# Relu² attention feeding a GELU feed-forward: attention regrouped into two slots per quad, one relu of each quad on VectorE, transposes of the head put later

## The chip, the cores and the metric

One core of a Trainium2 chip. The metric is the device time of one launch in microseconds (us), the median of several runs; lower is better. The engines are TensorE (PE), VectorE (DVE), ScalarE (ACT), GpSimd (POOL, here mostly the issuer of the loads) and SyncE (SP, the issuer of DMA transposes and of the stores).

## The reference

```python
# q, k, v: (8, 12, 448, 64) float32
scores = scale * np.matmul(q, k.transpose(0, 1, 3, 2))     # scale = 1/sqrt(64)
attn = np.maximum(scores, 0.0) ** 2 / S                    # S = 448
attn_out = np.matmul(attn, v)
x = attn_out.transpose(0, 2, 1, 3).reshape(8 * 448, 12 * 64)
h = x @ w_in                                               # (3584, 768) @ (768, 2048)
g = 0.5 * h * (1.0 + erf(h / np.sqrt(2)))
out = g @ w_out                                            # (3584, 2048) @ (2048, 768)
```

There is no softmax: the scores go through a relu and a square, so blocks of keys are independent until the value product sums them.

## The kernel before

**Tiles.** Everything is computed in bf16 with float32 sums. The 12 heads of a batch are three quads (`G = 3`, index g) of four heads. The 448 keys are seven blocks of 64 (`NK = 7`, index i). A *score step* `QK[b, g, i]` (`fn_qk`, L504) is four matmuls on 64x64 quarters of the array, one per head, into one PSUM tile `ps`. Its relu (`fn_relu`: L516 on ACT, L518 on DVE) makes `a_sq` out of it, and DVE squares that in place (L525). The *value product* `AV[b, g]` (L564) is 28 such matmuls over the seven squared blocks of a quad, into a PSUM tile `pav`, which two copies (L287 on DVE, L289 on ACT) put into `xT`. The feed-forward is made of atoms: F1 (`add_f1`, L611), six 128x128 matmuls into `psh` with a GELU on ACT after it (L623), and F2 (`add_f2`, L651), 16 matmuls into `pso`, copied by DVE to `osb` and stored by SP.

**Buffers.** `ps` and `pav` share a ring of three PSUM tiles (`w_pp`); `psh`, `pso` and the transposes' `tp` share two (`f_pp`).

**Order.** A planner in Python (`Scheduler`) fixes the order of instructions on each engine before the program is built, from modelled durations. Each operation has engines it may run on, dependencies, buffers that it needs and frees, and a bias; the earliest start plus bias is taken first. On the chip, each engine then runs its instructions in that order. The planner orders the head (batches 0 and 1) by itself. For the steady part (batches 2 to 7) PE's order is a list, `pe_q`: slots of attention, and between the slots feed-forward atoms. While batch b's attention runs, the atoms of *stage* b are F1 of batch b - 1 and F2 of batch b - 2, spread evenly over `per` slots. In `slots()`, a slot takes the value product that is ready, if any, and fills up with score steps: two units in the first slot, three in all others, so that 24 units of a batch make eight slots. The whole order of loads on POOL is a list too (`pool_q`).

**The head.** Batch 0 is done in two halves of the query columns. q and k of batches 0 and 1 are transposed on PE (`add_tq` L435, `add_tk` L410), those of later batches by DMA transposes, for which DVE first copies them into `pq` and `pk` (L371, L360). The q half that batch 0's second half needs is one load, issued after the first block of w_in. The transposes of that half have only a bias, `T_LATE`; those of batch 1 may not be planned before the last score step of batch 0's first half. On POOL a small copy, the gate (L479), waits until a batch's transposed q has landed before the next loads are issued; w_out's two loads stand behind the gate of batch 2.

**Copies for the next batch.** From batch 3 on, the `pk`/`pq` copies for batch b + 1 may start once the first score step of a given slot is done, `at(n)` with n counted from the stage's first slot: 5 for stage 2, 3 for stage 3, else 1. The DMA transposes of q's later parts wait for slot n + 1.

```python
sch.add(eng, fn_relu, [o1], need=("a",), frees=("w",), bias=bias, other=RELU_DVE)
...
for n, slot in enumerate(order):
    for kind, x in slot:
        pe_q.append(AV[x] if kind == "AV" else QK[x])
    if n < per * len(stage):
        ...
        while atoms and done < total * (n % per + 1) / per - 0.01:
```

Of the kernel before, what the change touches and what calls it, by code (L numbers as in the profile page):

```python
# [12 lines left out]
B, H, S, D = 8, 12, 448, 64  # L13
KC = 112
NC = S // KC
HC = NC // 2
HS = S // 2
KB = 64
NK = S // KB
NA = 14  # L20
HP = H // 2
G = H // 4
# [8 lines left out]
T_LATE = 0.2  # L31
# [11 lines left out]
DMA_LAT = 2.13  # L43
SWITCH = 0.09
LEAD = 5


def cols(half):
# [29 lines left out]
        return self.op.start  # L78


class Scheduler:


# [4 lines left out]
    def __init__(self, buffers):  # L88
# [2 lines left out]
        self.open, self.mode, self.dma = [], None, DMA_FREE  # L91
        self.landed = [0.0] * 8
        self.log = []

    def add(self, engines, fn, deps=(), **kw):
        op = Op(engines, fn, deps, **kw)
        self.open.append(op)
        return op
# [86 lines left out]
def kernel(  # L185
# [113 lines left out]
    def dma(fn, nbytes, deps=(), issues=1):  # L299
        op = sch.add((("POOL", 0.7 * issues, (nbytes, issues)),), lambda e: fn(), deps)  # L300
        pool_q.append(op)
        return op
# [4 lines left out]
    QK, SQ, AV, X, GL = {}, {}, {}, {}, {}  # L307
# [18 lines left out]
    def add_q(b, g0, g1, c0=0, c1=NC):  # L326
        o = dma(lambda: load_q(b, g0, g1, c0, c1), (g1 - g0) * 4 * KC * (c1 - c0) * 256, war(b))
        for g in range(g0, g1):
            for c in range(c0, c1):
                ld_q[b, g, c] = o  # L330

    def add_v(b, g0, g1):
        def fn():
            get_nat(b)
            nc.gpsimd.dma_start(vt[b][:, 2 * g0 : 2 * g1], kv_view(v, b, g0, g1))  # L335

        old = [o for (bb, *_), o in AV.items() if bb == b - 3]
        o = dma(fn, (g1 - g0) * 4 * S * 256, old)
        for g in range(g0, g1):
            ld_v[b, g] = [o]  # L340
# [6 lines left out]
    def add_win(i):  # L347
        m = sum(WINS[:i])
        c = slice(128 * m, 128 * (m + WINS[i]))
        o = dma(lambda: load_win(c), DM * 128 * WINS[i] * 4, issues=3)  # L350
        for x in range(m, m + WINS[i]):
            ld_win[x] = o
# [73 lines left out]
    def add_tq(b, g, c0=0, c1=NC, bias=T_BIAS, after=()):  # L426
        box, n = [], (c1 - c0) * KC

        def fn(e):
            tp = f_pp.tile([128, 2, n], BF16, tag="f", name="tp")  # L430
            box.append(tp)
            for j in range(2):
                for c in range(c0, c1):
                    for e in range(2):
                        nc.tensor.transpose(  # L435
                            tp[64 * e : 64 * e + 64, j, bass.ts(c - c0, KC)],
                            nq[b][:, 4 * g + 2 * e + j, bass.ts(c, D)],
                            ident[:KC, :KC],
                        )

        def fn2(e):
            copy(e, get_T(b)[0][:, 2 * g : 2 * g + 2, c0 * KC : c1 * KC], box[0])

        d = 0.125 * (c1 - c0)
        deps = [ld_q[b, g, c] for c in range(c0, c1)] + list(after)
        op = sch.add(
            (("PE", d, d + 0.22),), fn, deps, need=("f",), mode="T", bias=bias
        )
        ev = sch.add(e_copy(2 * n, 2), fn2, [op] + old_T(b), frees=("f",), bias=bias)
        for c in range(c0, c1):  # L450
            Tq[b, g, c] = (op, ev)
        return op
# [38 lines left out]
    def add_steps(todo, bias=0.0, dve=False):  # L491
        for blocks in todo:
            box = {}
            w = S if blocks[0][3] is None else HS
            used = w * len(blocks)

            def fn_qk(e_, blocks=blocks, box=box, w=w):
                ps = box["ps"] = w_pp.tile([128, 2, NB], F32, tag="w", name="ps")
                for x, (b, g, i, half) in enumerate(blocks):
                    qT, kT = get_T(b)  # L500
                    for e in range(2):
                        r = slice(64 * e, 64 * e + 64)
                        for j in range(2):
                            nc.tensor.matmul(  # L504
                                ps[64 * j : 64 * j + 64, e, x * w : x * w + w],
                                kT[r, g, i * 128 + 64 * j : i * 128 + 64 * j + 64],
                                qT[r, 2 * g + j, cols(half)],
                                start=True,
                                stop=True,
                            )  # L510

            def fn_relu(e_, box=box, used=used):
                box["a2"] = apool.tile([128, 2, S], BF16, tag="a", name="a_sq")
                ar, ps = box["a2"][:, :, :used], box["ps"][:, :, :used]
                if e_ == "ACT":
                    A.activation(ar, ps, AF.Relu, scale=c_att)  # L516
                else:
                    V.tensor_scalar(  # L518
                        ar, ps, c_att, 0.0,
                        op0=mybir.AluOpType.mult, op1=mybir.AluOpType.max,  # L520
                    )

            def fn_mul(e_, box=box, used=used):
                ar = box["a2"][:, :, :used]
                V.tensor_mul(box["a2"][:, :, :used], ar, ar)  # L525

            deps = []
            for b, g, i, half in blocks:
                cs = range(NC) if half is None else range(half * HC, half * HC + HC)
                deps += [Tk[b, g][1]] + [Tq[b, g, c][1] for c in cs]  # L530
            d = 0.19 * used / S
            o1 = sch.add((("PE", d, d + 0.24),), fn_qk, deps, need=("w",), mode="A", bias=bias)
            d = 0.19 + 0.00069 * 2 * used
            eng = (("ACT", d, d + 0.14),)
            if dve:
                d = 0.07 + 2 * used / 960
                eng += (("DVE", d, d + 0.12),)
            o2 = sch.add(
                eng, fn_relu, [o1], need=("a",), frees=("w",), bias=bias, other=RELU_DVE
            )  # L540
            d = 0.07 + used / 960
            o3 = sch.add((("DVE", d, d + 0.12),), fn_mul, [o2], bias=bias)
            for x, blk in enumerate(blocks):
                QK[blk] = o1
                SQ[blk] = (o3, box, x * w)
            for blk in blocks:
                if blk[2] == NK - 1:
                    add_av(blk, bias)
# [160 lines left out]
    def steps(b):  # L709
        return [((b, g, i, None),) for g in range(G) for i in range(NK)]  # L710
# [5 lines left out]
            tuple(x[n : n + 2]) for n in range(7, len(x), 2)  # L716
        ]

    def slots(todo, first):


        todo, ready, out = list(todo), [], []
        while todo or ready:
            slot, room = [], first if not out else 3
            new = []
            if ready:
                slot.append(("AV", ready.pop(0)))
            while todo and len(slot) < room:
                b, g, i, _ = todo.pop(0)[0]
                slot.append(("QK", (b, g, i, None)))  # L730
                if i == NK - 1:
                    new.append((b, g, None))
            ready += new
            out.append(slot)
        return out


    nc.scalar.dma_start(k32, kv_view(k, 0, 0, 1))
# [5 lines left out]
        out=ident, in_=ident, compare_op=mybir.AluOpType.not_equal, fill=1.0,  # L744
# [13 lines left out]
    for g in (1, 2):  # L758
        add_k(0, g, g + 1)
        add_q(0, g, g + 1, 0, HC)  # L760
        add_v(0, g - 1, g)
    add_v(0, 2, 3)
    add_win(0)
    add_q(0, 0, G, HC, NC)
    add_win(1)

    def landed(t):
# [20 lines left out]
        add_tk(0, g)  # L788
        add_tq(0, g, 0, HC)
    for g in range(G):  # L790
        add_tq(0, g, HC, NC, T_LATE)
    st0 = halves(0)
    add_steps(st0[:11], dve=True)
    add_steps(st0[11:], HALF_BIAS, True)
# [4 lines left out]
    add_load(1, 2, 3)  # L799
    add_win(4)  # L800
    for g in range(G):
        half = [order_only(QK[0, G - 1, NK - 1, 0])]
        add_tk(1, g, T_ONE, half)
        add_tq(1, g, bias=T_ONE, after=half)
    for m in range(0, KF, 2):
# [12 lines left out]
        add_f1(0, m, 1, bias=F1B_BIAS)  # L818


    todo = [x for b in range(2, B) for x in steps(b)]
    order = slots(todo, 2)
    first = [next((x for kind, x in sl if kind == "QK"), None) for sl in order]
    per = 8

    class at_slot:


        def __init__(self, n):
            self.key = first[n]  # L830

        @property
        def done(self):
            return QK[self.key].done
# [4 lines left out]
    stage = []  # L839
    add_load(3)  # L840
    for b in range(2, B):
        add_steps(steps(b))
        if b + 1 < B:

            n = per * (b - 2) + {2: 5, 3: 3}.get(b, 1)
            add_pk(b + 1, 0, G, after=at(n))
            add_pq(b + 1, 0, G, after=at(n))
            add_T_dma(b + 1, [at(n + (y >= 4)) for y in range(7)])
            if b + 2 < B:
                add_gate(b + 1)  # L850
                add_load(b + 2)
        x1, x2 = f1(b - 1), f2(b - 2)
        if b == 2:
            first_atoms = x1[:LEAD]
            stage.append(x1[LEAD:] + x2)
        else:
            stage.append(x2[:2] + mix(x1, x2[2:]))
    pe_q.extend(x[1] for x in first_atoms)
# [4 lines that stand above are left out]
            atoms = stage[n // per]  # L863
            if n % per == 0:
                total, done = sum(x[0] for x in atoms), 0.0
# [35 lines left out]
```

## Time and profile before

| what | us |
|---|---|
| device time, median of 3 runs | 399.45 |
| lowest and highest | 399.24, 400.35 |
| span in the profile | 398.9 |
| PE busy | 385.3 |
| ACT busy | 213.3 |
| DVE busy | 173.1 |

A page of the profile gives busy times of the engines over the span, rows of 40 equal slices, groups of equal instructions with their count, busy time and mean, and for each group what ended the idle time before it. Beside the page there are views of the same trace: a timeline (start, duration, engine, line, operation and tiles of merged instructions), windows (busy time of each engine in a stretch), waits, and a chain of waits. PE = matmuls, PEld = weight loads. Matmuls are pipelined and their ends are modelled; their starts are recorded.

### The profile page before, as it was taken

The page shows a single profiled execution, that of the slowest core. Times are in us where ns is not written, and L with a number is a line of the kernel's source. Part 1 is how long each engine was busy: PE and PEld are TensorE (multiplying, and loading weights), DVE is VectorE, ACT ScalarE, POOL GpSimd, SP SyncE. Part 2 cuts the span into 40 slices and gives each one's busy share as a digit, 9 for nine tenths or more (in the row PEclk, how much of TensorE's full clock was granted, in tenths as well). Part 3 has the DMA queues.
Part 4 walks back from the last instruction along what each step waited for, and adds up shares of the span by engine and source line. Part 5 has one row for each costly group of instructions (what it writes and reads, how often), then busy time and mean ns, then how long its engine had stood idle before and what let it go on. Part 6 is the DMA issues. An engine that isn't in the chain of part 4 may idle for free.

```text
span 398.9 us, 8136 instructions
## 1 busy us (share of the span) xinstructions
PE 385.3 (97%) x3497; PEld 215.8 (54%) x3497; DVE 173.1 (43%) x329; ACT 213.3 (53%) x323; POOL 45.2 (11%) x68
## 2 busy tenths in 40 slices
PE   7699999999999999999999999999999999999995
PEld 6477785455555555545555455545455555555552
DVE  3779961356544434634363433634343333110111
ACT  4878865774464654666546555556654646222200
POOL 8754204000200200020001000000000000000000
PEclk9879999999999999999999999999999999999998
DMA  9999966999895891897148921560111011110122
GB/s 178 187 203 204 199 100 109 212 203 217 140 204 115 118 200 35 155 158 116 41 90 131 187 60 41 113 106 2 41 30 51 2 41 41 39 28 14 41 79 79
DMA packets 69348, 42.95 MB, mean 108 GB/s; under 512 B 37696, under 2 KB 65728, under 8 KB 69312
## 3 DMA queue, kind: packets, MB, share of 16 engines
q0 software_dynamic: 30496, 22.47, 37.6%
q1 hardware_dynamic: 38544, 19.51, 23.4%
q8 instruction: 27, 0.44, 0.4%
q10 hardware_dynamic: 272, 0.46, 0.3%
q14 instruction: 9, 0.07, 0.1%
HBM read 45.61 MB, written 11.01 MB: 142 GB/s over the span
## 4 chain that ended last, share of the span: by engine, by line
PE 86%; DMA 4%; ACT 3%; DVE 2%; SPq 1%; POOL 1%; issue 1%; POOLq 0%; DVEq 0%; ACTq 0%
PE psh L611 36%; PE pso L651 35%; PE ps L504 8%; PE pav L564 7%; ACT a_sq L516 2%; DMA win_sb<-in_moe_w_in_dram 2%; DMA nk<-in_k_dram 2%; SPq L467 1%; DMA qT<-pq 1%; POOL v_sb L335 1%; DVE xT L287 0%; DVE a_sq L525 0%; DVE osb L287 0%; POOL nk L320 0%; PE tp L410 0%
## 5 line engine op out<-in xcount | busy, mean ns | idle before, releaser
L516 ACT ACTIVATE a_sq<-ps 128x896 bf16<-128x896 f32 (+1 forms) x161 | 140.7, 920 | 35.7 <-PE ps L504 35.7
L611 PE MATMUL psh<-xT,win_sb 128*128 128x448 bf16 (+1 forms) x864 | 156.1, 332 | 0.4 <-DVE osb L287 0.4
L651 PE MATMUL pso<-wout_sb,h_sb 128*128 128x384 bf16 x896 | 152.7, 326 | 0.0
L525 DVE TENSOR_TENSOR a_sq<-a_sq 128x896 bf16<-128x896 bf16 (+1 forms) x169 | 103.0, 621 | 104.9 <-ACT a_sq L516 104.8
L651 PEld LDWEIGHTS <-h_sb 128*128 128x128 bf16 x896 | 86.2, 98 | 63.6 <-issue 6.9
L611 PEld LDWEIGHTS <-win_sb 128*128 128x128 bf16 x864 | 80.7, 98 | 68.5 <-issue 13.6
L623 ACT ACTIVATE h_sb<-psh 128x448 bf16<-128x448 f32 x128 | 70.5, 551 | 68.2 <-PE psh L611 68.1
L287 DVE COPY osb<-pso 128x384 f32<-128x384 f32 x56 | 31.1, 556 | 77.3 <-PE pso L651 77.3
L504 PE MATMUL ps<-qT,kT 64*64 64x448 bf16 (+1 forms) x756 | 46.5, 339 | 2.4 <-ACT a_sq L516 1.6
L289 ACT CAST xT<-pav 128x448 bf16<-128x448 f32 (+1 forms) x26 | 12.9, 496 | 48.7 <-DVE xT L287 47.8
L564 PE MATMUL pav<-a_sq,v_sb 64*64 64x448 bf16 (+1 forms) x756 | 37.9, 339 | 0.4 <-ACT a_sq L516 0.4
L504 PEld LDWEIGHTS <-kT 64*64 64x64 bf16 x756 | 19.2, 107 | 22.1 <-issue 15.6
L287 DVE CAST xT<-pav 128x448 bf16<-128x448 f32 (+1 forms) x28 | 15.8, 566 | 29.7 <-PE pav L564 29.3
L564 PEld LDWEIGHTS <-v_sb 64*64 64x64 bf16 x756 | 20.3, 110 | 15.4 <-issue 7.6
L479 POOL COPY gate<-qT 128x4 bf16<-128x4 bf16 x5 | 0.9, 186 | 159.8 <-DMA qT<-pq 159.8
L236 POOL DMA_DIRECT2D nq<-in_q_dram x14 | 11.6, 827 | 1.5 <-DMA win_sb<-in_moe_w_in_dram 0.6
L335 POOL DMA_DIRECT2D v_sb<-in_v_dram x14 | 10.6, 761 | 3.3 <-DMA win_sb<-in_moe_w_in_dram 1.7
L320 POOL DMA_DIRECT2D nk<-in_k_dram x13 | 10.0, 769 | 5.0 <-DVE xT L287 2.0
L518 DVE TENSOR_SCALAR a_sq<-ps 128x896 bf16<-128x896 f32 x8 | 8.6, 1085 | 0.7 <-PE ps L504 0.7
L371 DVE COPY pq<-nq 112x512 bf16<-112x512 bf16 x36 | 8.3, 287 | 0.3 <-DMA nq<-in_q_dram 0.3
L435 PE MATMUL tp<-ident,nq 112*64 112x112 bf16 x96 | 4.2, 230 | 2.3 <-DMA nq<-in_q_dram 1.3
L360 DVE COPY pk<-nk 128x896 bf16<-128x896 bf16 x18 | 6.1, 386 | 0.0
(24 smaller groups left out, 42.3 us busy)
## 6 DMA issues: line engine op xcount, KB each, us to landing
nk<-in_k_dram POOLq DMA_DIRECT2D x5, 672.0 KB, 6.6
nq<-in_q_dram POOLq DMA_DIRECT2D x5, 672.0 KB, 9.3
v_sb<-in_v_dram POOLq DMA_DIRECT2D x5, 672.0 KB, 12.7
wout_sb<-in_moe_w_out_dram POOLq DMA_DIRECT2D x2, 1536.0 KB, 14.9
out_dram<-osb SPq DMA_DIRECT2D x8, 336.0 KB, 3.2
out_dram<-osb SPq DMA_DIRECT2D x8, 288.0 KB, 2.7
v_sb<-in_v_dram POOLq DMA_DIRECT2D x9, 224.0 KB, 8.0
out_dram<-osb SPq DMA_DIRECT2D x8, 240.0 KB, 2.7
```

Source lines behind the costliest of these rows:

```text
L236: nc.gpsimd.dma_start(nq[b][:, 4 * g0 : 4 * g1, c0 * D : c1 * D], q_view(b, g0, g1, c0, c1))
L287: V.tensor_copy(dst, src)
L289: A.copy(dst, src)
L320: nc.gpsimd.dma_start(nk[b][:, 2 * g0 : 2 * g1], kv_view(k, b, g0, g1))
L335: nc.gpsimd.dma_start(vt[b][:, 2 * g0 : 2 * g1], kv_view(v, b, g0, g1))
L504: nc.tensor.matmul(ps[64 * j : 64 * j + 64, e, x * w : x * w + w], kT[r, g, i * 128 + 64 * j : i * 128 + 64 * j + 64], qT[r, 2 * g + j, co ...
L516: A.activation(ar, ps, AF.Relu, scale=c_att)
L525: V.tensor_mul(box["a2"][:, :, :used], ar, ar)
L564: nc.tensor.matmul(pav[0][o2 : o2 + 64, e, :w], vt[b][r, 2 * g + e, bass.ts(i, D)], box["a2"][r, e, o : o + w], start=(i == 0), stop=(i == ...
L611: nc.tensor.matmul(ph[:, x * n : x * n + n], win_sb[:, kd, bass.ts(m + x, 128)], xT[b][:, kd, c], start=(kd == 0), stop=(kd == KD - 1),)
L623: A.activation(hT[b // 2][:, m : m + nm, o + c.start : o + c.stop], box[0][:, :S].rearrange("p (x n) -> p x n", x=nm), AF.Gelu,)
L651: nc.tensor.matmul(po[:, :ND], hT[pr][:, kf, bass.ts(t, 128)], wout_sb[:, kf, bass.ts(n, ND)], start=(kf == 0), stop=(kf == KF - 1),)
```

## The change

Steady attention gets two slots for each quad. The first holds two score steps, the value product of the quad before, and two more score steps; the second holds the other three score steps. A batch so has six slots (`per = 2 * G`) where it had eight. With five PSUM tiles asked for in one slot from a ring of three, the relu of a quad's second score step (`DVE_STEPS = (1,)`) is given to DVE in the steady part, so that it runs beside the first relu on ACT. The points from which the next batch's copies may start are moved with the slots.

In the head, q's second half for batch 0 is loaded before the first block of w_in; its transposes may be planned only from the start of the value product of quad 1, and those of batch 1 only from the start of the value product of quad 2 (class `later` reads a start time that is set during planning).

```diff
+DVE_STEPS = (1,)
+TQ_AFTER = 1
...
-            if dve:
-                d = 0.07 + 2 * used / 960
+            d = 0.07 + 2 * used / 960
+            if dve is True:
                 eng += (("DVE", d, d + 0.12),)
+            elif dve and blocks[0][2] in DVE_STEPS:
+                eng = (("DVE", d, d + 0.12),)
...
-    def slots(todo, first):
-        todo, ready, out = list(todo), [], []
-        while todo or ready:
-            slot, room = [], first if not out else 3
-            new = []
-            if ready:
-                slot.append(("AV", ready.pop(0)))
-            while todo and len(slot) < room:
-                b, g, i, _ = todo.pop(0)[0]
-                slot.append(("QK", (b, g, i, None)))
-                if i == NK - 1:
-                    new.append((b, g, None))
-            ready += new
-            out.append(slot)
-        return out
+    def slots(first, last):
+        out, done = [], None
+        for b in range(first, last):
+            for g in range(G):
+                x = [("QK", (b, g, i, None)) for i in range(NK)]
+                out.append(x[:2] + ([("AV", done)] if done else []) + x[2:4])
+                out.append(x[4:])
+                done = (b, g, None)
+        return out + [[("AV", done)]]
...
+    add_q(0, 0, G, HC, NC)
     add_win(0)
-    add_q(0, 0, G, HC, NC)
     add_win(1)
...
-        add_tq(0, g, HC, NC, T_LATE)
+        add_tq(0, g, HC, NC, T_LATE, [later(lambda: AV[0, TQ_AFTER, 0].start)])
...
-        half = [order_only(QK[0, G - 1, NK - 1, 0])]
+        half = [order_only(AV[0, G - 1, 0])]
...
-    per = 8
+    per = 2 * G
...
-        add_steps(steps(b))
+        add_steps(steps(b), dve=1)
...
-            n = per * (b - 2) + {2: 5, 3: 3}.get(b, 1)
+            n = per * (b - 2) + {2: 2, 3: 2}.get(b, 1)
```

More of the change, by code (lines that the diff above doesn't have):

```diff
@@ L78, in done, with __init__ @@
         return self.op.start
+class later:
+    def __init__(self, time):
+        self.time = time
+    @property
+    def done(self):
+        return self.time()
 class Scheduler:
@@ L818 @@
         add_f1(0, m, 1, bias=F1B_BIAS)
-    todo = [x for b in range(2, B) for x in steps(b)]
-    order = slots(todo, 2)
+    order = slots(2, B)
     first = [next((x for kind, x in sl if kind == "QK"), None) for sl in order]
-    per = 8
+    per = 2 * G
     class at_slot:
```

## The prediction

> **What bounds the kernel now.** I read the page first, then the matmul engine's timeline over a stretch of steady work, then the head in the timeline and the windows, then the queue of loads.
>
> From the page:
>
> ```profile
> PE 385.3 (97%) x3497; PEld 215.8 (54%) x3497; DVE 173.1 (43%) x329; ACT 213.3 (53%) x323; POOL 45.2 (11%) x68
> ...
> PEclk9879999999999999999999999999999999999998
> ...
> L516 ACT ACTIVATE a_sq<-ps 128x896 bf16<-128x896 f32 (+1 forms) x161 | 140.7, 920 | 35.7 <-PE ps L504 35.7
> ...
> L518 DVE TENSOR_SCALAR a_sq<-ps 128x896 bf16<-128x896 f32 x8 | 8.6, 1085 | 0.7 <-PE ps L504 0.7
> ```
>
> PE is busy nearly everywhere, ACT and DVE about half the time. So after the head only PE time counts: what PE executes, what it loses when it changes between attention and feed-forward matmuls, and its few waits. The clock row dips once, in the head. The PE timeline of the steady part (start, duration, group):
>
> ```profile
> 102.39 1.52 PE L564 MATMUL pav<-a_sq,v_sb 64*64 64x448 bf16 x28
> 104.34 0.57 PE L504 MATMUL ps<-qT,kT 64*64 64x448 bf16 x8 [0.43 <-DMA qT<-pq]
> ...
> 113.45 2.43 PE L611 MATMUL psh<-xT,win_sb 128*128 128x448 bf16 x12
> 115.81 0.76 PE L504 MATMUL ps<-qT,kT 64*64 64x448 bf16 x12
> ...
> 121.48 1.52 PE L564 MATMUL pav<-a_sq,v_sb 64*64 64x448 bf16 x28
> 122.83 0.55 PE L504 MATMUL ps<-qT,kT 64*64 64x448 bf16 x8
> 123.31 1.31 PE L611 MATMUL psh<-xT,win_sb 128*128 128x448 bf16 x6
> ...
> 128.98 2.44 PE L611 MATMUL psh<-xT,win_sb 128*128 128x448 bf16 x12
> 131.26 2.76 PE L651 MATMUL pso<-wout_sb,h_sb 128*128 128x384 bf16 x16
> 133.95 0.76 PE L504 MATMUL ps<-qT,kT 64*64 64x448 bf16 x12
> 134.65 2.44 PE L611 MATMUL psh<-xT,win_sb 128*128 128x448 bf16 x12
> ...
> 175.23 0.38 PE L504 MATMUL ps<-qT,kT 64*64 64x448 bf16 x4 [0.16 <-ACT a_sq L516]
> ```
>
> Starts are exact, ends modelled, so I subtract starts. The same 12 F1 matmuls take 2.36 us ahead of attention (113.45 to 115.81) and 2.28 us ahead of feed-forward (128.98 to 131.26); 16 F2 matmuls 2.69 (131.26 to 133.95) against 2.61 where F1 follows. Entering attention costs 0.08 us. Three score steps take 0.70 (133.95 to 134.65), two 0.48 (122.83 to 123.31): 0.21 each and about 0.06 for leaving. A slot thus costs 0.14 us beyond its work. The value product takes 1.35 (121.48 to 122.83). Three exceptions: 0.6 us where scores waited for transposed q (1.95 in place of 1.35 at 102.39), and 0.35 us where a third step waited for a relu (the slot from 174.50 to 175.55 took 1.05 in place of 0.70; the one at 267.73 likewise).
>
> The head, from the timeline and the windows (after the span: busy of PE, PEld, DVE, ACT, POOL, clock, DMA):
>
> ```profile
> 16.85 0.58 PE L435 MATMUL tp<-ident,nq 112*64 112x112 bf16 x16 [1.28 <-DMA nq<-in_q_dram]
> ...
> 20.83 0.96 PE L410 MATMUL tp<-ident,nk 128*64 128x128 bf16 x14 [1.48 <-DMA nk<-in_k_dram]
> ```
>
> ```profile
> 20.00:24.00 4.00, 3.17 (x60) 2.62 (x62) 1.49 (x4) 1.97 (x3) 2.38 (x4) 0.50 1.26 204
> ```
>
> PE, which runs in order, stood 2.8 us on transposes whose data had not landed. From 16 to 24 us its clock is 0.71 and then 0.50, and DVE and ACT starve (1.49 and 1.97 us busy of 4). From 24 us on PE is full (4.00 of 4 in the next window).
>
> ```profile
> 64.34 0.18 POOL L479 COPY gate<-qT 128x4 bf16<-128x4 bf16 x1 [21.06 <-DMA qT<-pq]
> 64.57 1.78 POOL L259 DMA_DIRECT2D wout_sb<-in_moe_w_out_dram  x2
> ```
>
> Here is a second clock for the head: the w_out loads are issued only when batch 2's q transposes have landed, and take up to 18.2 us (the tile view of wout_sb), so the second half lands near 65.5 + 18.2 = 83.7. F2 first runs at 82.35, and its ninth matmul, the first that reads that half, is due at 82.35 + 8 x 2.60 / 16 = 83.65. There is no slack at all.
>
> **What the Trainium skill says.** TensorEngine Tiling (Array Packing), Key Properties: changing the tiling mode drains TensorE. The trace agrees (64*64 against 128*128 groups, 0.14 us a round trip). TensorE: Matmul & The Clock Gate, Part 1: PE falls to half clock after a window of about 3.4 us with too little work and needs a busy one to recover; the trace's 0.50 stretch fits. VectorE: DVE Perf Modes, Mode 2×_2P — use both read ports for one tensor: PSUM has one DVE read port, so the two-port rate is out; the trace has 1085 ns for the relu from PSUM.
>
> **The change part by part.**
>
> *Fewer slots.* Before: 126 score steps and 18 value products of batches 2 to 7 make 144 units, one slot of two, then three each, and the last product alone: 49 slots. After: two per quad, 36, and one alone: 37. Twelve round trips go: 12 x 0.14 = 1.7 us, all on PE. The work within is the same. A score step beside a value product is the same 64*64 mode; no cost.
>
> *The steady waits.* The two relu waits came where only 12 F1 matmuls (2.4 us) lay between two slots; now each stretch of feed-forward holds a sixth of a stage, over 4.5 us, so 0.7 us goes. The q wait of 0.6 us: copies for batch 3 are now due from slot 2, not 5, but their loads land only near 90 us (pq stood at 90.6 for nq), and the value product no longer runs ahead of the first score step. I count half gone. Together -1.0 us.
>
> *The new wait.* A full slot now takes five PSUM tiles (ps, ps, pav, ps, ps) from a ring of three. Step 3 needs the first relu done, step 4 the second. ACT's timing in the slot that starts at 163.50:
>
> ```profile
> 163.60 0.54 ACT L623 ACTIVATE h_sb<-psh 128x448 bf16<-128x448 f32 x1 [1.67 <-PE psh L611]
> 164.04 1.72 ACT L516 ACTIVATE a_sq<-ps 128x896 bf16<-128x896 f32 x2
> ```
>
> With a gelu ahead, relu 1 runs from +0.54 to +1.46. Step 3 is due at 2 x 0.21 + 1.35 = +1.77: 0.3 us of slack. Relu 2 on ACT would end at +2.26, with step 4 due at +1.98: 0.3 us late each time. On DVE it starts when step 2 is done (about +0.64) and ends at +1.73: 0.25 us early. That is what the DVE share is for. Queued behind it on DVE are the squares and the pav copies; the next slot that needs them is 4.5 us away. An osb copy ahead of it (0.56 us from about +0.1) costs nothing. Only a burst of pk/pq copies (0.3 to 0.5 us each) can push it. Bounds: 0 if none do, 18 x 0.4 = 7 us if each slot has one more DVE operation in the way. I take 0.3.
>
> *ACT and DVE loads.* 18 relus of 0.92 us leave ACT and 18 of 1.09 go to DVE; both engines stay near half busy, worth nothing on PE.
>
> *The head.* q's second half is loaded ahead of the first w_in block, so it lands earlier; its transposes go behind the value product of quad 1, batch 1's behind that of quad 2. So PE need not stand at 16.85 and 20.83. But the value product at 17.37 could not finish before its squares, done at 17.5, so the first wait is worth little; the second, and work at half clock until 24, are worth more. Bounds for PE's lead at 24 us: 0 to 2.8 of waits plus some 3 of half clock. I take 2.5. It is kept only so far as the w_out landing moves too. The copies that start that chain (pk, 52.62) sit behind squares on a DVE that is full from 36 to 52, so a fuller DVE at 17 to 24 should bring them forward, but only down to the landing of batch 2's loads, near 50. Kept: 0 to 2.5; I take 1.5.
>
> Sum: 399.45 - 1.7 - 1.0 + 0.3 - 1.5 = 395.55, rounded to 395.5.
>
> **The rivals.**
> - *The head's lead is lost at w_out.* PE arrives early at F2 and waits out its whole lead. For: the zero slack. Against: DVE idles at 20 to 24 and can start the chain earlier. 399.45 - 2.4 = 397.0.
> - *The head gives all.* No cold stretch and the chain moves 2.5 to 4 us: 393.
> - *PSUM becomes the bound.* Relu 2 starts a DVE operation late in most full slots: 18 x 0.3 to 0.4 = 5.4 to 7, less 2.7 gained: 402. For: only 0.25 us of slack. Against: DVE is under half busy.
> - *The new order of the head is worse.* Transposes later mean scores of half 1 and the copies of batch 2 later, w_out 2 to 3 us later: 399.4.
>
> **How the numbers follow.** As forecast 0.45; lead lost at w_out 0.22; head gives all 0.12; head worse 0.11; PSUM bound 0.10. Faster is the first three, 0.79, less 0.01 for the near side of 397; same 0.09 and slower 0.13 share the last two and what lies between. The range, 392.6 to 399.4, takes in the first three whole and the edge of the fourth.
>
> **What would show it.** Right: about 37 entries into attention after 62 us; full slots of 2.2 to 2.3 us with no wait at their third and fourth step; idle at 16 to 21 us nearly gone; F2 starting as w_out lands. Wrong: score steps waiting on a_sq of DVE or ACT in most full slots, DVE standing on nk or nq near 85 to 91 us, or the gate at 64.34 opening later.

## The result and the profile after

The changed kernel takes 396.81 us (median of 4 runs, 396.01 to 397.48) against 399.46 before: a ratio of 0.9929, 95% interval 0.9903 to 0.9955. (A ratio is formed from the single runs, so it is not exactly the quotient of the medians.) The span in the profile went from 398.9 to 395.7 us. In the changed kernel line numbers are 7 to 14 higher: score steps are L516, value products L578, F1 L625, F2 L665, the relus L528 on ACT and L530 on DVE.

From the page of the changed kernel, the rows shown of before:

```profile
PE 381.9 (97%) x3497; PEld 218.1 (55%) x3497; DVE 187.5 (47%) x346; ACT 200.5 (51%) x306; POOL 45.2 (11%) x68
...
PEclk9989999999999999999999999999999999999999
...
L528 ACT ACTIVATE a_sq<-ps 128x896 bf16<-128x896 f32 x143 | 124.7, 916 | 48.8 <-PE ps L516 48.8
...
L530 DVE TENSOR_SCALAR a_sq<-ps 128x896 bf16<-128x896 f32 x26 | 28.3, 1090 | 37.5 <-PE ps L516 37.5
```

Eighteen relus moved from ACT (161 to 143) to DVE (8 to 26). Neither engine became a bound. PE's busy time fell by 3.4 us with the same 3497 matmuls. Modelled ends reach over the gap at a change of mode (in the kernel before, the F1 group of 113.45 ends at 115.88, after the score step of 115.81 has started), so fewer changes of mode show as less busy time.

The PE timeline of the changed kernel (start, duration, group; in brackets the idle time before it):

```profile
65.04 0.76 PE L516 MATMUL ps<-qT,kT 64*64 64x448 bf16 x12
...
66.55 0.38 PE L516 MATMUL ps<-qT,kT 64*64 64x448 bf16 x4 [0.75 <-ACT a_sq L528]
...
103.45 0.57 PE L516 MATMUL ps<-qT,kT 64*64 64x448 bf16 x8 [0.94 <-DMA qT<-pq]
...
120.36 0.57 PE L516 MATMUL ps<-qT,kT 64*64 64x448 bf16 x8
...
120.77 1.49 PE L578 MATMUL pav<-a_sq,v_sb 64*64 64x448 bf16 x28
...
122.09 0.55 PE L516 MATMUL ps<-qT,kT 64*64 64x448 bf16 x8
...
122.57 2.44 PE L625 MATMUL psh<-xT,win_sb 128*128 128x448 bf16 x12
```

The full slot runs without a wait from 120.36 to 122.57: two steps in 0.41, the value product in 1.32, two steps in 0.48. Two steps followed by more attention take 0.41, two followed by feed-forward 0.48. The three waits in attention that are new or larger are the fourth step of the very first slot, which has no value product in its middle (66.55, 0.92 us counted from start to start), batch 3's first step, for its transposed q (103.45, 1.01 us), and the fourth step of one full slot (93.42, 0.34 us). On ACT and DVE the same slot shows the two relus side by side:

```profile
120.91 0.91 ACT L528 ACTIVATE a_sq<-ps 128x896 bf16<-128x896 f32 x1
120.99 1.09 DVE L530 TENSOR_SCALAR a_sq<-ps 128x896 bf16<-128x896 f32 x1 [0.79 <-PE ps L516]
```

They end at 121.82 and 122.08; steps 3 and 4 start at 122.09 and 122.28. And the queue of loads:

```profile
64.49 0.18 POOL L491 COPY gate<-qT 128x4 bf16<-128x4 bf16 x1 [21.15 <-DMA qT<-pq]
64.72 1.78 POOL L271 DMA_DIRECT2D wout_sb<-in_moe_w_out_dram  x2
```

The gate opens where it did before (64.34), and F2 first runs at 82.47 (82.35 before). So all of the gain between these two profiles was made after F2 began.

To size it I summed the distances between matmul starts from the first steady score step to the last matmul of the last value product, in the three traces that differ in their number of slots (the third is run e4 below):

| us (number of entries) | before | change | e4 |
|---|---|---|---|
| the whole stretch | 273.1 | 270.6 | 274.2 |
| F1 and F2 matmuls at 0.1893 and 0.1625 each | 212.6 | 212.6 | 212.6 |
| entering attention, beyond that | 4.48 (48) | 3.36 (36) | 5.04 (54) |
| attention and leaving it, waits taken out | 53.66 | 52.12 | 54.39 |
| waits for batch 3's q | 0.60 | 1.01 | 0.98 |
| waits for a relu or a square | 0.66 | 1.26 | 0.21 |
| waits inside feed-forward | 1.17 | 0.31 | 1.02 |

From before to the change, a round trip is worth (1.12 + 1.54) / 12 = 0.22 us. That is 2.66 us for twelve, and the waits together are about as large as before (2.43 against 2.58).

### The profile page after: what moved, and what is told of

Same layout as the page of the kernel before. It is cut to its first block, busy times and chain, and to the rows that moved or that the text cites. A ratio compares the mean times of both kernels' runs of the same rounds, so it can differ in the third digit from the quotient of the medians.

```text
span 395.7 us, 8091 instructions
## 1 busy us (share of the span) xinstructions
PE 381.9 (97%) x3497; PEld 218.1 (55%) x3497; DVE 187.5 (47%) x346; ACT 200.5 (51%) x306; POOL 45.2 (11%) x68
## 4 chain that ended last, share of the span: by engine, by line
PE 79%; DMA 10%; ACT 3%; DVE 3%; SPq 2%; POOL 1%; issue 1%; POOLq 0%
PE pso L665 33%; PE psh L625 32%; DMA nq<-in_q_dram 9%; PE ps L516 7%; PE pav L578 6%; ACT a_sq L528 2%; SPq L479 2%; DMA qT<-pq 1%; DVE a_sq L537 1%; PE tp L447 1%; POOL nk L332 1%; DVE a_sq L530 1%; ACT h_sb L637 1%; DVE xT L299 0%; POOL wout_sb L271 0%
## 5 line engine op out<-in xcount | busy, mean ns | idle before, releaser
L625 PE MATMUL psh<-xT,win_sb 128*128 128x448 bf16 (+1 forms) x864 | 155.9, 334 | 0.0
L665 PE MATMUL pso<-wout_sb,h_sb 128*128 128x384 bf16 x896 | 151.7, 326 | 0.0
L528 ACT ACTIVATE a_sq<-ps 128x896 bf16<-128x896 f32 x143 | 124.7, 916 | 48.8 <-PE ps L516 48.8
L537 DVE TENSOR_TENSOR a_sq<-a_sq 128x896 bf16<-128x896 bf16 (+1 forms) x169 | 100.6, 618 | 55.6 <-ACT a_sq L528 55.6
L665 PEld LDWEIGHTS <-h_sb 128*128 128x128 bf16 x896 | 86.3, 98 | 62.3 <-issue 5.6
L625 PEld LDWEIGHTS <-win_sb 128*128 128x128 bf16 x864 | 82.1, 98 | 66.4 <-issue 9.2
L516 PE MATMUL ps<-qT,kT 64*64 64x448 bf16 (+1 forms) x756 | 47.4, 339 | 3.8 <-ACT a_sq L528 2.1
L530 DVE TENSOR_SCALAR a_sq<-ps 128x896 bf16<-128x896 f32 x26 | 28.3, 1090 | 37.5 <-PE ps L516 37.5
L578 PE MATMUL pav<-a_sq,v_sb 64*64 64x448 bf16 (+1 forms) x756 | 36.6, 329 | 0.8 <-ACT a_sq L528 0.8
L516 PEld LDWEIGHTS <-kT 64*64 64x64 bf16 x756 | 19.1, 106 | 24.4 <-issue 17.9
L578 PEld LDWEIGHTS <-v_sb 64*64 64x64 bf16 x756 | 21.1, 107 | 12.4 <-issue 2.1
L762 PE MATMUL spin<-zero 128*128 128x128 bf16 x45 | 4.6, 299 | 1.0 <-DVE zero L749 1.0
```

What stands on the lines that cost most here:

```text
L516: nc.tensor.matmul(ps[64 * j : 64 * j + 64, e, x * w : x * w + w], kT[r, g, i * 128 + 64 * j : i * 128 + 64 * j + 64], qT[r, 2 * g + j, co ...
L530: V.tensor_scalar(ar, ps, c_att, 0.0, op0=mybir.AluOpType.mult, op1=mybir.AluOpType.max,)
L578: nc.tensor.matmul(pav[0][o2 : o2 + 64, e, :w], vt[b][r, 2 * g + e, bass.ts(i, D)], box["a2"][r, e, o : o + w], start=(i == 0), stop=(i == ...
L625: nc.tensor.matmul(ph[:, x * n : x * n + n], win_sb[:, kd, bass.ts(m + x, 128)], xT[b][:, kd, c], start=(kd == 0), stop=(kd == KD - 1),)
L665: nc.tensor.matmul(po[:, :ND], hT[pr][:, kf, bass.ts(t, 128)], wout_sb[:, kf, bass.ts(n, ND)], start=(kf == 0), stop=(kf == KF - 1),)
```

## The experiments

Theory A: the gain is the twelve round trips, at 0.22 us each; the head's edits give nothing that lasts, since F2 can't run before w_out has landed; the DVE relu is what makes the full slot possible. Theory B: PE's work and waits simply add up, so 0.8 us of the gain is the head's. Each ratio is to the kernel before on the same chip, with its 95% interval.

**e1: the steady part alone.**

```diff
-    add_q(0, 0, G, HC, NC)
     add_win(0)
+    add_q(0, 0, G, HC, NC)
...
-        add_tq(0, g, HC, NC, T_LATE, [later(lambda: AV[0, TQ_AFTER, 0].start)])
+        add_tq(0, g, HC, NC, T_LATE)
...
-        half = [order_only(AV[0, G - 1, 0])]
+        half = [order_only(QK[0, G - 1, NK - 1, 0])]
```

> The change with the three edits of the head undone (order of the q load, both transposes put later); the two slots per quad, the DVE relu and the copy points stay. Theory A (the gain is made after F2 begins; the head's lead is lost because F2 can't run before w_out has landed, near 83.6 us): about 397.0, within 0.5 us of the changed kernel's 396.8, and F2 begins at 82 to 83.5 us as in both kernels. Theory B (the head's 0.8 us lead at the first steady score step is kept to the end): 397.6, that is 0.8 us over the changed kernel.

Measured: 396.63 us, 0.9919 (0.9894 to 0.9944). The whole gain is there without the head's edits. What I had not expected: PE reached the first steady score step at 64.39, though up to there PE, ACT and DVE run the same instructions in the same order as the kernel before, whose profile has 65.82. The gate opened earlier too:

```profile
63.06 0.18 POOL L491 COPY gate<-qT 128x4 bf16<-128x4 bf16 x1 [19.57 <-DMA qT<-pq]
...
64.39 0.76 PE L516 MATMUL ps<-qT,kT 64*64 64x448 bf16 x12
```

F2 then began at 81.82, a little before the 82 us of the expectation. So the change's 65.04 is no lead that could be read from one pair of profiles. What goes with these times is the clock between 20 and 24 us, the third figure from the end, here in the change and in e1 (the same row of the kernel before has 0.50):

```profile
20.00:24.00 4.00, 3.09 (x64) 2.34 (x65) 2.23 (x4) 2.50 (x4) 2.80 (x4) 0.77 1.25 204
...
20.00:24.00 4.00, 3.00 (x98) 2.39 (x98) 2.38 (x6) 2.71 (x5) 2.64 (x4) 1.00 1.27 205
```

Twelve of the profiles have the same loads ahead of the gate. In three of them the clock of this window is 0.50 to 0.77 (before, the change, e10), and the gate opens at 64.05 to 64.49; in the other nine it is 0.99 or 1.00, and the gate opens at 62.95 to 63.72, with the old head (63.06 in e1, 62.95 in e11) as with the new. The second half of w_out landed 19.0 to 19.7 us after the gate in all twelve. With one profile for each run this is a correlation and not a proof, but it leaves no sign that the order of the head moves the gate.

**e2: the head alone** (the kernel before with the three edits of e1 the other way round).

> The kernel before with the three edits of the head alone. Theory A: the first steady score step comes some 0.8 us earlier, F2's ninth matmul then waits for w_out, and the time is that of before within 0.4 us (399.1 to 399.8). Theory B: 398.7, 0.8 us under before.

Measured: 399.40 us, 0.9995 (0.9980 to 1.0010). No gain that this run can tell; theory B's 0.8 us (0.9980) lies at the very edge of the interval. In its timeline the first steady step comes at 63.98, and then:

```profile
80.51 1.46 PE L663 MATMUL pso<-wout_sb,h_sb 128*128 128x384 bf16 x8
82.67 1.46 PE L663 MATMUL pso<-wout_sb,h_sb 128*128 128x384 bf16 x8 [0.70 <-DMA wout_sb<-in_moe_w_out_dram]
```

The ninth F2 matmul should follow the first by 8 x 0.1625 = 1.30 us and comes 2.16 us after it. PE arrived early and stood 0.86 us for w_out's second half. No interval alone excludes 0.8 us, which is 0.2%. Together the comparisons of old and new head (e1 with the change and e10, e2 with before, e11 below with e7 and e12) put its worth between -0.4 and 0.3 us.

**e3: the second relu back on ACT.**

```diff
-        add_steps(steps(b), dve=1)
+        add_steps(steps(b))
```

> The change, with the second relu of each quad in the steady part left on ACT. Theory A (a relu on DVE beside the first on ACT is what keeps the fourth score step of a full slot from waiting): relu 2 ends about 2.3 us after the slot's start where the fourth step is due at 1.9, so 17 full slots wait 0.4 to 0.5 us each: about 7 us more, 403 to 405, slower than before. Rival (ACT gets there in time, or PE has slack): within 0.5 us of 396.8.

Measured: 402.64 us, 1.0074 (1.0052 to 1.0095): slower than before. Its timeline in a full slot, ACT's two relus and then PE:

```profile
136.97 1.72 ACT L528 ACTIVATE a_sq<-ps 128x896 bf16<-128x896 f32 x2
...
138.15 0.36 PE L516 MATMUL ps<-qT,kT 64*64 64x448 bf16 x4
...
138.74 0.38 PE L516 MATMUL ps<-qT,kT 64*64 64x448 bf16 x4 [0.23 <-ACT a_sq L528]
```

The fourth step starts 0.58 us after the third in place of 0.18, once the second relu has ended at 138.69. That wait of 0.4 us stands in 15 of the 18 slots, 0.3 in two more and 0.9, as in the change, in the first. The 17 add up to 6.6 us; the wait for batch 3's q shrank by 0.7, and the time grew by 5.8. It is the wait for a PSUM tile that costs, and not ACT's load: ACT was 53% busy before with these relus on it.

**e4: three slots per quad.**

```diff
-                out.append(x[:2] + ([("AV", done)] if done else []) + x[2:4])
+                out.append(x[:2] + ([("AV", done)] if done else []))
+                out.append(x[2:4])
                 out.append(x[4:])
...
-    per = 2 * G
+    per = 3 * G
...
-            n = per * (b - 2) + {2: 2, 3: 2}.get(b, 1)
+            n = per * (b - 2) + {2: 3, 3: 3}.get(b, 1)
```

> The change with each quad in three slots (two steps and the value product, two steps, three steps): 18 round trips more between attention and feed-forward. By the sums over both traces a round trip costs 0.22 us: 18 x 0.22 = 4.0, less 0.3 for a relu wait that goes, 400.5. By the price in the prediction, 0.14 us: 2.5 less 0.3, 399.0.

Measured: 400.04 us, 0.9999 (0.9985 to 1.0014), 3.2 us over the change and 3.4 over e1 on the same chip. By the table, 18 more round trips cost (1.68 + 2.27) / 18 = 0.22 each, 3.9 us, and its waits are 0.4 us shorter. The price of 0.22 stands, that of 0.14, or 2.5 us for 18, does not. The price can also be read from single slots that differ in one step alone:

```profile
113.96 0.76 PE L516 MATMUL ps<-qT,kT 64*64 64x448 bf16 x12
114.65 1.31 PE L625 MATMUL psh<-xT,win_sb 128*128 128x448 bf16 x6
...
126.43 0.57 PE L516 MATMUL ps<-qT,kT 64*64 64x448 bf16 x8
126.94 3.39 PE L625 MATMUL psh<-xT,win_sb 128*128 128x448 bf16 x17
```

Three steps between feed-forward groups take 0.69 us and two take 0.51 (0.694 and 0.505 as medians over the trace), so a step is 0.19 and a visit costs 0.126 beyond its steps. With 0.093 for entering that is 0.22.

**e5: an F2 atom ahead of batch 3's first score steps.**

```diff
         else:
+            if b == 3:
+                stage[0].append(x2.pop(0))
             stage.append(x2[:2] + mix(x1, x2[2:]))
```

> The change with the first F2 atom of stage 3 put at the end of stage 2, ahead of batch 3's first score steps. Theory A (PE stands 1.0 us there for batch 3's transposed q, while ready feed-forward work lies behind it): the wait is gone, 1.0 us less than the changed kernel, 395.8. Rival (the transposes, or the loads behind the gate, move later with it, and the time is lost again later): within 0.3 us of 396.8.

Measured: 394.93 us, 0.9893 (0.9870 to 0.9916). The wait of 1.0 us is gone from its trace (the step at 103.93 follows F2 with no idle time) and nothing took its place. The time is 1.9 us under the change's, but it was taken on another chip; by the ratios (0.9893 against 0.9929 and, in e10, 0.9918) it is 1.0 to 1.4. The two profiles differ by 2.1 us, because the relu wait of 0.34 us is gone as well and the first steady step comes 0.75 us earlier: the head of this execution had no half-clock stretch, and its gate opened at 63.56.

**e6: an F1 atom inside the first slot.**

```diff
-        for kind, x in slot:
+        for y, (kind, x) in enumerate(slot):
+            if (n, y) == (0, 2):
+                pe_q.append(stage[0].pop(0)[1])
```

> The change with one F1 atom put between the second and third score step of the very first steady slot, which has no value product to cover the first relu (there PE stood 0.9 us). Theory A: that wait goes at the price of one more round trip (0.2 us), but F2 then comes to its ninth matmul before w_out has landed and waits there for the 0.7 us that were won: no change, 396.5 to 397.1. Theory B (PE's work and waits simply add up): 0.7 us less, 396.1.

Measured: 397.12 us, 0.9950 (0.9929 to 0.9971): no gain. The relu wait went, and the time reappears at F2:

```profile
80.64 1.47 PE L665 MATMUL pso<-wout_sb,h_sb 128*128 128x384 bf16 x8
82.50 1.46 PE L665 MATMUL pso<-wout_sb,h_sb 128*128 128x384 bf16 x8 [0.39 <-DMA wout_sb<-in_moe_w_out_dram]
```

1.86 us in place of 1.30: 0.56 us for w_out. Batch 3's q then cost 1.3 us in place of 1.0. This is theory A's point: ahead of w_out's landing, PE time that is saved is not saved.

**e7 and e12: both edits; e11: both, with the old head.**

> Both edits, the F2 atom ahead of batch 3 and the split first slot. Theory A: only the first is worth anything, 1.0 us, 395.8. Theory B: both add up, 1.7 us, 395.1.

> Run e7 (F2 atom ahead of batch 3, split first slot) with the three edits of the head undone. Theory A (the head's order is worth nothing, F2's start being set by w_out and PE's full speed in the head by where the clock's window falls): 394.75 as e7, within 0.5 us. Theory B: 0.8 us over e7, 395.5.

> Run e7 once more. e7's six times lay within 0.2 us and its profile had no half-clock stretch in the head; e11, the same with the old head, had one, and spread over 2 us. If the new head keeps the clock up, this run again has no such stretch, 394.7, and a small spread; if that was chance, it has one in some executions and 394.7 to 396.4, as e11.

Measured: e7 394.75 us, 0.9888 (0.9867 to 0.9909); e11 396.06, 0.9896 (0.9873 to 0.9919); e12 395.23, 0.9895 (0.9868 to 0.9922). The three ratios agree with each other and with e5's 0.9893: the second edit and the head's order are worth nothing that these runs can tell. (In microseconds e11 is 1.3 over e7, but the kernel before took 0.6 longer on its chip.) In e7 and e12 the ninth F2 matmul still stands 0.6 and 1.0 us for w_out. In e12 the clock from 12 to 16 us was 0.58, and its times spread over 1.6 us as e11's did over 2.1, so e7's narrow spread was no mark of the new head. With the fill alone (e5) or with both edits the kernel is some 0.3% under the change, the fastest found.

**e8: half of w_out loaded ahead of the gate; e9: with more F1 atoms ahead of the first score step.** Both carry the two edits of e7.

```diff
-    add_gate(2)
     add_wout(0)
+    add_gate(2)
     add_wout(1)
...
-LEAD = 5
+LEAD = 7
```

The last line is e9's alone.

> Both edits, and the first half of w_out loaded ahead of batch 2's gate, while the loads stand idle. Theory A (w_out's landing sets when F2 can begin): F2 no longer waits for w_out, batch 3's q lands some 7 us earlier, and the time is 1.7 to 2.2 us under the changed kernel, 394.6 to 395.1, unless the load slows the transposes of batch 2. Rival (it does): the gate opens 2 us or more later, PE stands at the first steady score step, and the time is 396 or more.

Measured: 396.62 us, 0.9941 (0.9918 to 0.9965). The rival was right: the load slowed batch 2's transposes, the first on SP's queue and then PE, waiting for them:

```profile
53.37 6.54 SPq L471 DMA_TRANSPOSE kT<-pk  x3
```

```profile
66.66 0.57 PE L516 MATMUL ps<-qT,kT 64*64 64x448 bf16 x8 [1.71 <-DMA qT<-pq]
```

The same three issues took 4.17 us in the change. From there on the trace has no wait longer than 0.1 us for w_out, q or a relu; what was won later was paid here. The gate opened at 66.67, over 2 us later than in any profile without this load.

> Run e8 with seven in place of five F1 atoms ahead of the first steady score step. Theory A (e8 lost only the 1.7 us that PE stood there for the slower transposes, and ready F1 work can stand in its place): the wait goes, 1.7 us less than e8, 394.9, the same as e7 within 0.5 us. Rival (the later gate costs elsewhere too): 396 or more.

Measured: 397.06 us, 0.9952 (0.9925 to 0.9978), in single runs up to 400.56. The F1 atoms did fill the wait; another took its place. DVE, PE:

```profile
81.80 0.40 DVE L372 COPY pk<-nk 128x896 bf16<-128x896 bf16 x1 [3.54 <-DMA nk<-in_k_dram]
82.11 1.08 DVE L530 TENSOR_SCALAR a_sq<-ps 128x896 bf16<-128x896 f32 x1
...
83.25 0.59 PE L516 MATMUL ps<-qT,kT 64*64 64x448 bf16 x4 [2.75 <-DVE a_sq L530]
...
83.77 2.59 PE L665 MATMUL pso<-wout_sb,h_sb 128*128 128x384 bf16 x8
```

By the planner's modelled landing time a `pk` copy of batch 3 stood here; its k landed 3.5 us after DVE came to it. The second relu of a full slot was queued behind it on DVE, and PE stood behind that. Then PE ran at half clock: eight F2 matmuls in 2.59 us, where they take 1.46.

**e10: the change again.**

> The change itself, beside e11 and e9 on one chip. Theory A: 396.8 within 0.5 us, 1.4 to 2.0 us over e11, since its waits for batch 3's q are still there.

Measured: 396.80 us, 0.9918 (0.9892 to 0.9943), with the same waits as in the first profile (0.9 us in the first slot, 0.3 in the slot at 93 us, 1.25 at batch 3). It is only 0.7 us over e11 (0.9 by the ratios), less than the 1.4 to 2.0 expected.

## Why the prediction was right, point by point

It forecast 395.5 in a range of 392.6 to 399.4; the time is 396.81.

- *Round trips, -1.7 us.* The right step, sized too small: 2.66 us. I compared two steps behind a value product (0.48) with three behind feed-forward (0.70) and took the difference, 0.21, as a step. The second group holds a slower first step after the change of mode as well. A step is 0.19, leaving costs about 0.10 and not 0.06, and the slower first step 0.02 (a value product takes 1.35 us behind feed-forward and 1.32 behind a score step); with 0.09 for entering that is 0.21 to 0.22. e4 measured the same.
- *Steady waits, -1.0 us.* Half right. Both relu waits of before (0.66) went, and so did 0.9 us inside feed-forward that I had left alone (0.52 of it one wait for an `osb` copy, at 207.8). The q wait grew from 0.60 to 1.01: no value product runs ahead of batch 3's first step any longer, and its loads stand behind w_out's.
- *The new wait, +0.3 us.* The slack of full slots held in 16 of 17; the one with `pq` copies ahead of its relu lost 0.34. I overlooked the first slot, with four steps and no value product: 0.92. Together 1.26. e3 shows what the DVE relu is for: without it the kernel is slower than before.
- *ACT and DVE loads, 0.* Right.
- *The head, -1.5 us.* This term fell. Of the two waits the one for q went, but the one for k fell only from 1.48 to 1.28 us, and a new one of 0.45 for q followed it. The first steady step came 0.8 us earlier in the one pair of profiles, but e1 came earlier still without the edits. I had let the copies that start the gate's chain move forward with the new head. They did not: the first `pk` copy starts at 53.05 against 52.62, and the gate opens at 64.49 against 64.34. Where the gate did open earlier, it did so with either head (e1 and e11 as well as e2). And e2 and e6 show the lead of PE lost at w_out. That was the first rival, and its 397.0 is nearer than my forecast.

The sum of what the two profiles show is -2.66 for the round trips, +0.15 for waits and -0.78 at the first steady step: 3.29 us, as the spans differ by 3.2. The first two alone give 2.5, and the medians differ by 2.65; e1, e2 and e11 give the head's edits no worth that can be seen.

That the number came so close is in part luck. Three terms were off by a microsecond or more: the round trips brought 1.0 us more than forecast, the new wait cost 1.0 us more, and these two cancel; what is left of the error, 1.3 us, is nearly the head's 1.5.

What stays open is whether the new head runs at full clock more often. TensorE: Matmul & The Clock Gate, Part 1, in the Trainium skill says that the window in which activity is judged runs freely, so that the same kernel meets it at another phase each time. These runs agree that the same order of work gets different clocks: in the windows view from 6 to 28 us the clock is 0.84 in the profile before and 0.92 in e1 and e11, all with the old head; with the new head it is 0.92 in five profiles and 1.00 in six. Three against eleven is too few to tell the heads apart.

## What to carry to other kernels

A change of tiling mode on TensorE has a price that can be read from starts alone, but only by comparing groups that differ in one thing: the same number of matmuls with the same neighbour on one side. Fewer and longer visits pay as long as the ring of PSUM buffers turns over inside the visit, and where it does not turn over in time, a second engine for one of the evictions helps, even when neither engine is near full (here 6 us on PE for 18 relus). Before speeding up an early stage, look for a transfer that sets when the next stage may begin: time won ahead of it turns into a wait.

## What the runs showed of the hardware

- A round trip between 128x128 and 64x64 matmuls cost 0.22 us here: 0.093 on entering the 64x64 mode, 0.126 for leaving and a slower first step together.
- The half-clock stretch in the head is 6.8 us long in the profile before, 3.4 us in seven others and absent in six, also between heads with the same order of work. Six times of e7 lay within 0.2 us, those of e12, the same kernel on another chip, within 1.7 (394.65 to 396.29).
- In mid-kernel, during one stall of PE of 2.75 us (e9), the clock fell to half at 82.67 and stayed there for 3.4 us. In the 3.41 us up to that point PE had been busy for 1.24.
- DMA transposes beside a load of w_out took 6.54 us (e8) and 7.05 (e9) for three issues, against 4.17 in the change and 3.99 in e7.
